# Softmax normaliser by a vector reciprocal, and the causal mask by a vector copy, in a recurrent attention and gMLP kernel

## The chip, the cores and the metric

The kernel runs on one core of a Trainium2 chip. The time is that of one execution on the device, in microseconds (us), as the median of several runs. Engine names in the profile: PE is TensorE (matmuls), PEld its weight loads, DVE is VectorE, ACT is ScalarE, POOL is GpSimd, SP is SyncE, which here only issues DMAs. PSUM is the memory that TensorE writes its products to; it has eight banks of 128 partitions by 512 float32.

## The reference

Two blocks run one after the other on x of shape (2048, 512). The first is attention over segments of 32 rows with a memory of 8 rows that is carried from segment to segment, so the 64 segments can only be computed in order:

```python
for s in range(64):
    h = concat([mem, xs])                      # 8 + 32 rows of 512
    q, k, v = h @ Wq, h @ Wk, h @ Wv           # 32 heads of 128
    scores = where(mask, q k^T * scale, -1e9)  # 40 x 40 per head
    o = (softmax(scores) @ v) @ Wo
    mem, out[s] = o[:8], o[8:]
```

The mask lets every key through for the 8 memory rows and is causal for the others. The second block is a gated MLP: a layer norm, a product with `w_in`, GELU, a layer norm of one half, a product with the 2048x2048 matrix `w_sp` over the rows, a gate, and a product with `w_out`. Both blocks add to their input.

## The kernel before

All instructions are recorded by an `Emitter` with one list for each engine. The order in which the Python code calls `pe`, `act`, `dve`, `pool` and `sp` is the order on that engine, and waits are derived from the tokens that an instruction reads and writes, among them one token for each PSUM bank (`PB(bank)`). So the order of work is written out by hand in the loop over `s`.

A step of that loop is one segment. The 32 heads are handled in two halves, `b` = 0 and 1. In one half, four groups of 32 partitions hold four heads each. A step goes like this:

- `QK` (L481) computes queries and keys of a half, `QK_evac` copies them from PSUM by ScalarE (L488) and transposes them by VectorE (L494 for queries, L497 for keys).
- `S_half` puts the scores of a half into bank 0 or 1 (`SBK`). It begins with four matmuls of an identity with the mask (L511), which start the accumulation. Sixteen matmuls for the segment's own keys (L520) and four for the memory's keys (L526) add to it.
- `sm_exp` (L534) computes E = exp(scale * score + 44) by ScalarE.
- `sm_sums` (L541, L546) multiplies E by a block of ones, so that every row of a head's block holds the sum over the keys, in the same bank (columns 224 to 383).
- `sm_ln` (L553) and `sm_rcp` (L557) form the reciprocal of these sums by ScalarE, as exp(-ln(sum)) with scale factors.
- `sm_norm` (L561, L566) multiplies E by it on VectorE, in two instructions.
- `V_half` (L575) computes the values of a half, in four quarters of four matmuls; `V_evac` copies them from PSUM, by VectorE for half 0 (L584), by ScalarE for half 1 (L582).
- Then a filler group follows, a piece of work for a later stage (L411, L430 or L735), which all steps have but one.
- `PV_half` (L592, L598) multiplies values and probabilities, half 0 then half 1, into banks 0, 1, 6 and 7; `cT_evac` (L611, L613) copies the result out. Below, PV(0) and PV(1) are the two halves.
- `Wo` (L625) applies the output matrix, and `mem_out` (L649, L654) turns the first 8 rows into the memory for the next step's `QK`. `WoX_mm` (L676) does the remaining rows of earlier segments.

`qx_copy` (L504) runs once in each step on GpSimd, behind the scores, and serves as a clock for the steps. In step 0 the values of the memory part are computed as well (`start_v`), between the scores and `V_half`.

Of the kernel before, what the change touches and what calls it, by code (L numbers as in the profile page):

```python
# [9 lines left out]
ACT = mybir.ActivationFunctionType  # L10
ALU = mybir.AluOpType
# [158 lines left out]
def fast_path(nc, st, keep, A_x, A_mem0, A_Wq, A_Wk, A_Wv, A_Wo, A_seg_len, B_w_in, B_w_sp, B_b_sp, B_w_out, out):  # L170
# [9 lines left out]
    DC = D // 128  # L180
# [7 lines left out]
    scale = float(DH) ** -0.5  # L188
    EPS = 1e-5
    SHIFT = 44.0  # L190
    NEG = -1.0e30
    RBIAS = 44.42
    LNS = 2.0 ** -64
    RK = math.exp(-RBIAS)

    em = Emitter(n_dma_sems=40)

# [27 lines left out]
    E_sb = sb("E_sb", [128, 2, 224], BF)  # L225
    R_sb = sb("R_sb", [128, 2, 160], F32)
# [7 lines left out]
    ident = sb("ident", [128, 128], BF)  # L234
    mask = sb("mask", [128, 224], BF)
# [30 lines left out]
    def PB(b):  # L266
        return ("ps", b)
# [4 lines left out]
    def pe(fn, **k):  # L272
        return em.add("pe", fn, **k)

    def act(fn, **k):
        return em.add("act", fn, **k)

    def dve(fn, **k):
        return em.add("dve", fn, **k)

    def pool(fn, **k):
        return em.add("pool", fn, **k)
# [40 lines left out]
    def late_consts():  # L323
        pool(lambda e: e.memset(ones[:], 0.0), writes=["ones"])
        pool(lambda e: e.memset(Sc[:], 0.0), writes=["Sc"])
        pool(lambda e: e.memset(mask[:], 0.0), writes=["mask"])
        for c in range(4):
            q = slice(32 * c, 32 * c + 32)
            pool(lambda e, q=q: e.memset(ones[q, q], 1.0), writes=["ones"])
            pool(lambda e, q=q: e.affine_select(out=G_sb[q, :], in_=onesrc[q, 0:M], pattern=[[-1, M]], compare_op=ALU.is_equal,  # L330
                                                fill=0.0, base=0, channel_multiplier=1), reads=["onesrc"], writes=["G"])
            pool(lambda e, q=q: e.affine_select(out=F_sb[q, :], in_=onesrc[q, 0:32], pattern=[[-1, 32]], compare_op=ALU.is_equal,
                                                fill=0.0, base=-M, channel_multiplier=1), reads=["onesrc"], writes=["F"])
            pool(lambda e, q=q: e.affine_select(
                out=Sc[q, :].rearrange("p (s r) -> p s r", r=32)[:, :, XM:32], in_=onesrc[q, 0:32].rearrange("p (s r) -> p s r", r=8),
                pattern=[[-8, 4], [-1, 8]], compare_op=ALU.is_equal, fill=0.0, base=0, channel_multiplier=1),
                reads=["onesrc"], writes=["Sc"])
            m1 = mask[q, 0:160].rearrange("p (g t) -> p g t", t=40)[:, :, 16:40]
            pool(lambda e, m1=m1: e.affine_select(out=m1, in_=m1, pattern=[[0, 4], [1, 24]], compare_op=ALU.is_ge,
                                                  fill=NEG, base=8, channel_multiplier=-1), reads=["mask"], writes=["mask"])  # L340
            m2 = mask[q, 160:224].rearrange("p (g t) -> p g t", t=16)
            pool(lambda e, m2=m2: e.affine_select(out=m2, in_=m2, pattern=[[-8, 4], [0, 16]], compare_op=ALU.is_ge,
                                                  fill=NEG, base=0, channel_multiplier=1), reads=["mask"], writes=["mask"])
            pool(lambda e, m2=m2: e.affine_select(out=m2, in_=m2, pattern=[[8, 4], [0, 16]], compare_op=ALU.is_ge,
                                                  fill=NEG, base=7, channel_multiplier=-1), reads=["mask"], writes=["mask"])
            m3 = m2[:, :, 0:8]
            pool(lambda e, m3=m3: e.affine_select(out=m3, in_=m3, pattern=[[8, 4], [1, 8]], compare_op=ALU.is_ge,
                                                  fill=NEG, base=0, channel_multiplier=-1), reads=["mask"], writes=["mask"])
# [136 lines left out]
    def QK_evac(s, b, mi):  # L485
        bank = QKB[(b, mi)]
        tb = mi
        act(lambda e: e.activation(out=Tst[:, tb, :].rearrange("p (hp i r) -> p hp i r", i=32, r=2),  # L488
                                   in_=ps[:, bank, :].rearrange("p (hp r i) -> p hp i r", r=2, i=32), func=ACT.Copy),
            reads=[PB(bank)], writes=[("T", tb)])  # L490
        src = Tst[:, tb, :].bitcast(U32)
        if mi == 0:
            dst = QT[:, b, :, :, :].rearrange("p hp q r -> p (hp q r)").bitcast(U32).rearrange("p (hp q) -> p hp q", hp=8)[:, :, 8:40]
            dve(lambda e: e.transpose(out=dst, in_=src), reads=[("T", tb)], writes=[("QT", b)])  # L494
        else:
            dst = KT[:, b, :, :, :].rearrange("p hp q r -> p (hp q r)").bitcast(U32)
            dve(lambda e: e.transpose(out=dst, in_=src), reads=[("T", tb)], writes=[("KT", b)])  # L497

    def qx_copy(s):
# [4 lines left out]
        pool(lambda e: e.tensor_copy(out=dst, in_=src), reads=[("QTx", buf, 0, i) for i in range(8)],  # L504
             writes=[("QTe", 0), ("QTe", 1)])

    def S_half(s, b):
        bank = SBK[b]
        for c in range(4):
            q = slice(32 * c, 32 * c + 32)  # L510
            pe(lambda e, q=q, c=c: e.matmul(ps[q, bank, 0:224], lhsT=ident[:, q], rhs=mask[:, :], start=True, stop=False,  # L511
                                            skip_group_check=True, tile_position=(0, 32 * c)),
               reads=["ident", "mask"], writes=[PB(bank)])
        j = s % CK
        buf = (s // CK) % 2
        rd = [("QT", b), ("KT", b), ("QTe", b)]
        for g in range(4):
            for c in range(4):
                hp, r = 2 * c + g // 2, g % 2
                pe(lambda e, hp=hp, r=r, c=c, g=g: e.matmul(  # L520
                    ps[32 * c:32 * c + 32, bank, g * 40:(g + 1) * 40], lhsT=KT[:, b, hp, :, r], rhs=QT[:, b, hp, :, r],
                    start=False, stop=(g == 3), skip_group_check=True, tile_position=(0, 32 * c)),
                    reads=rd, writes=[PB(bank)])
        for c in range(4):
            h0 = 16 * b + 4 * c
            pe(lambda e, c=c, h0=h0: e.matmul(  # L526
                ps[32 * c:32 * c + 32, bank, 160:224], lhsT=QTx[buf][:, 1, j, h0:h0 + 4, :].rearrange("p h k -> p (h k)"),
                rhs=QT[:, b, 2 * c:2 * c + 2, 0:16, :].rearrange("p hp q r -> p hp r q"),
                start=False, stop=True, skip_group_check=True, tile_position=(0, 32 * c)),
                reads=rd + [("QTx", buf, 1, i) for i in range(8)], writes=[PB(bank)])  # L530
# [17 lines left out]
                                            skip_group_check=True, tile_position=(0, 32 * c)),  # L548
               reads=[("Ex", b), "ones"], writes=[PB(bank)])

    def sm_ln(b):
        bank = SBK[b]
        act(lambda e: e.activation(out=R_sb[:, b, :], in_=ps[:, bank, 224:384], func=ACT.Ln, scale=LNS),  # L553
            reads=[PB(bank)], writes=[("R", b)])

    def sm_rcp(b):
        act(lambda e: e.activation(out=R_sb[:, b, :], in_=R_sb[:, b, :], func=ACT.Exp, scale=-1.0, bias=RBIAS),  # L557
            reads=[("R", b)], writes=[("R", b)])

    def sm_norm(b):  # L560
        dve(lambda e: e.scalar_tensor_tensor(out=E_sb[:, b, 0:160], in0=R_sb[:, b, :], scalar=RK, in1=E_sb[:, b, 0:160],  # L561
                                             op0=ALU.mult, op1=ALU.mult),
            reads=[("R", b), ("E", b)], writes=[("E", b)])
        ev = E_sb[:, b, 160:224].rearrange("p (g q) -> p g q", q=16)
        rv = R_sb[:, b, :].rearrange("p (g q) -> p g q", q=40)[:, :, 0:16]
        dve(lambda e: e.scalar_tensor_tensor(out=ev, in0=rv, scalar=RK, in1=ev, op0=ALU.mult, op1=ALU.mult),  # L566
            reads=[("R", b), ("Ex", b)], writes=[("Ex", b)])

    def V_half(s, b, dcs=range(DC)):
# [31 lines left out]
                start=False, stop=True, skip_group_check=True, tile_position=(32 * c, 0)),  # L601
                reads=[("Vx", xb), ("Ex", b)], writes=[PB(PVB[c])])

    UNSC = 2.0 ** -64


    def cT_evac(c, eng):
# [288 lines left out]
    for s in range(NSEG):  # L896
# [16 lines left out]
        QK(s, 0, 1, (0, 1))  # L913
        QK(s, 0, 0, (2, 3))
        QK_evac(s, 0, 0)
        QK(s, 0, 1, (2, 3))
        QK_evac(s, 0, 1)
        for mi in range(2):
            QK(s, 1, mi)
            lastop["qk"[mi]] = em.by_eng["pe"][-1]  # L920
            QK_evac(s, 1, mi)
        if s == 0:
            for n in range(2):
                start_v(n)
# [3 lines left out]
            for n in range(2, 4):  # L928
                start_v(n)
        V_half(s, 0)  # L930
        V_evac(0, "dve")
        sm_sums(0)
        sm_ln(0)
        S_half(s, 1)
        lastop["s"] = em.by_eng["pe"][-1]
        sm_exp(1)
        sm_rcp(0)
        if s == 0:
            for n in range(4, 8):
                start_v(n)  # L940
        V_half(s, 1, (0, 1, 2))
        sm_sums(1)
        sm_ln(1)
        sm_rcp(1)
        V_half(s, 1, (3,))
        lastop["v"] = em.by_eng["pe"][-1]
        if s == NSEG - 1:
            sp(lambda e: e.dma_start(w_in1, winr[:, :, 0:FH]), writes=["w_in1"], after=[lastop["s"], lastop["x"]])
            xn2T_dma(11, [lastop["s"], lastop["x"]])
            z2_back(0, 7, lastop["v"])  # L950
        V_evac(1, "act")
        sm_norm(0)
        sm_norm(1)
        if s + 1 < NSEG:
            qx_copy(s + 1)
            lastop["x"] = em.by_eng["pool"][-1]
# [1037 lines left out]
```

## Time and profile before

| what | value |
|---|---|
| median of 3 runs | 885.25 us |
| lowest and highest run | 884.95 and 886.3 us |
| the profiled execution, its own time | 887.59 us |
| the profiled execution, span of its instructions | 885.8 us |
| mean granted TensorE clock in it | 0.994 |

The profile is of one execution, and its span leaves out a little at both ends, so its own time is above its span and, here, the median of the unprofiled runs is slightly below the span. In the rows of a timeline the columns are: start in us, duration in us, engine, line, operation, output and inputs, and how many instructions were merged into the row; in brackets how long the engine was idle before it and what ended that. The duration of a merged row reaches from the first start to the last end. In a row of a group the numbers behind the bar are the total busy time in us and the mean duration in ns.

### The profile page before, as it was taken

What the parts mean: (1) busy time and instruction counts of PE and PEld (TensorE: products, weight loads), DVE (VectorE), ACT (ScalarE), POOL (GpSimd) and SP (SyncE); (2) the same over time, 40 slices, a digit from 0 to 9 for tenths busy, and PEclk for the clock granted to TensorE, in tenths of its full rate; (3) what the DMA queues carried; (4) which work ended last, traced back from release to release, by engine and by line L of the source; (5) the groups of instructions that cost most, each with busy time, mean ns of one, the idle gap of its engine ahead of it and who ended that gap; (6) DMA issues with size and microseconds to landing.
All of it is one profiled execution on the core that took longest, in us unless ns stands there. A gap on an engine that the chain in (4) does not pass through costs nothing.

```text
span 885.8 us, 46595 instructions
## 1 busy us (share of the span) xinstructions
PE 858.6 (97%) x21446; PEld 488.5 (55%) x21453; DVE 487.6 (55%) x1128; ACT 457.3 (52%) x1147; POOL 110.6 (12%) x280
## 2 busy tenths in 40 slices
PE   6889999999999999999999999999999998999997
PEld 6645555565566655656565555555555543444443
DVE  3445556565556556565655565556555557364343
ACT  2346565666665656666665666466665575400000
POOL 1420111111111111010101011111101013200000
PEclk9999999999999999999999999999999999999999
DMA  9962232123320311211312121523222299032101
GB/s 320 377 177 63 64 57 61 44 59 63 60 58 25 84 46 32 65 45 52 60 43 52 46 66 47 102 69 78 73 62 67 62 244 333 2 101 76 62 13 38
DMA packets 109210, 76.35 MB, mean 86 GB/s; under 512 B 64104, under 2 KB 94512, under 8 KB 109008
## 3 DMA queue, kind: packets, MB, share of 16 engines
q1 hardware_dynamic: 108496, 73.04, 30.1%
q8 instruction: 170, 2.79, 1.3%
q14 instruction: 32, 0.26, 0.1%
q0 software_dynamic: 192, 0.20, 0.1%
q10 hardware_dynamic: 320, 0.07, 0.0%
HBM read 41.75 MB, written 20.91 MB: 71 GB/s over the span
## 4 chain that ended last, share of the span: by engine, by line
PE 94%; DVE 2%; issue 1%; DMA 1%; POOL 1%; ACT 0%; DVEq 0%
PE f_ps L481 26%; PE f_ps L625 13%; PE f_ps L575 12%; PE f_ps L1099 11%; PE f_ps L411 7%; PE f_ps L676 4%; PE f_ps L592 3%; PE f_ps L430 3%; PE f_ps L1188 3%; PE f_ps L1092 2%; PE f_ps L735 2%; PE f_ps L520 2%; PE f_ps L541 1%; PE f_ps L511 1%; PE f_ps L649 1%
## 5 line engine op out<-in xcount | busy, mean ns | idle before, releaser
L481 PE MATMUL f_ps<-f_arena,f_hT 128*32 128x512 bf16 x4096 | 240.3, 380 | 0.5 <-issue 0.2
L488 ACT ACTIVATE f_Tst<-f_ps 128x512 bf16<-128x512 f32 x256 | 145.9, 596 | 78.1 <-PE f_ps L481 77.9
L481 PEld LDWEIGHTS f_ps<-f_arena,f_hT 128*32 128x32 bf16 x4096 | 92.9, 96 | 104.0 <-ACT f_hT L654 32.7
L575 PE MATMUL f_ps<-f_arena,f_hT 128*32 128x512 bf16 x2048 | 140.4, 378 | 0.0
L625 PE MATMUL f_ps<-f_arena,f_cT 128*32 128x256 bf16 x4096 | 129.2, 274 | 0.9 <-ACT f_cT L611 0.8
L625 PEld LDWEIGHTS f_ps<-f_arena,f_cT 128*32 128x32 bf16 x4096 | 101.2, 97 | 21.7 <-ACT f_cT L611 18.7
L494 DVE STREAM_TRANSPOSE f_QT<-f_Tst 128x256 uint32<-128x256 uint32 x128 | 57.0, 446 | 91.7 <-ACT f_Tst L488 91.7
L1099 PE MATMUL f_ps<-f_arena 128*128 128x512 bf16 x448 | 100.9, 382 | 0.0
L613 DVE TENSOR_SCALAR f_cT<-f_ps 128x320 bf16<-128x320 f32 x128 | 56.9, 487 | 41.2 <-PE f_ps L598 41.2
L1099 PEld LDWEIGHTS f_ps<-f_arena 128*128 128x128 bf16 x448 | 44.1, 99 | 53.9 <-issue 2.2
L497 DVE STREAM_TRANSPOSE f_KT<-f_Tst 128x256 uint32<-128x256 uint32 x128 | 57.0, 445 | 29.1 <-ACT f_Tst L488 26.4
L411 PE MATMUL f_ps<-f_hTe,f_arena 128*128 128x128 bf16 x1024 | 68.0, 225 | 4.0 <-DVE f_arena L422 2.9
L611 ACT ACTIVATE f_cT<-f_ps 128x320 bf16<-128x320 f32 x128 | 49.0, 435 | 38.4 <-PE f_ps L598 38.4
L411 PEld LDWEIGHTS f_ps<-f_hTe,f_arena 128*128 128x128 bf16 x1024 | 60.3, 101 | 14.1 <-issue 9.5
L504 POOL COPY f_QT<-f_arena 128x256 bf16<-128x256 bf16 x64 | 30.7, 479 | 298.2 <-PE f_ps L526 298.1
L561 DVE SCALAR_TENSOR_TENSOR f_E_sb<-f_R_sb,f_E_sb 128x160 bf16<-128x160 f32 x128 | 41.7, 325 | 46.2 <-ACT f_R_sb L557 46.2
L642 DVE CAST f_part<-f_ps 128x256 bf16<-128x256 f32 x64 | 27.2, 425 | 68.9 <-PE f_ps L625 68.9
L553 ACT ACTIVATE f_R_sb<-f_ps 128x160 f32<-128x160 f32 x128 | 39.0, 305 | 37.9 <-PE f_ps L546 37.9
L575 PEld LDWEIGHTS f_ps<-f_arena,f_hT 128*32 128x32 bf16 x2048 | 45.2, 95 | 21.1
L1105 DVE TENSOR_TENSOR f_arena<-f_ps,f_arena 128x512 f32<-128x512 f32 x28 | 19.3, 690 | 60.7 <-PE f_ps L1099 60.7
L654 ACT ACTIVATE f_hT<-f_ps 128x16 bf16<-128x16 f32 x126 | 23.2, 184 | 55.1 <-PE f_ps L649 54.7
L633 POOL COPY f_cTx<-f_cT 128x256 bf16<-128x256 bf16 x64 | 25.6, 400 | 197.1 <-DVE f_cT L613 197.1
(113 smaller groups left out, 1165.8 us busy)
## 6 DMA issues: line engine op xcount, KB each, us to landing
wT_d<-f_wst SPq DMA_DIRECT2D x32, 256.0 KB, 2.3
f_arena<-wT_d SPq DMA_DIRECT2D x32, 256.0 KB, 5.1
f_arena<-in_A_Wq_dram SPq DMA_DIRECT2D x4, 1024.0 KB, 8.8
f_arena<-in_A_Wk_dram SPq DMA_DIRECT2D x4, 1024.0 KB, 14.2
f_arena<-in_A_Wv_dram SPq DMA_DIRECT2D x4, 1024.0 KB, 14.8
f_arena<-in_A_Wo_dram SPq DMA_DIRECT2D x4, 1024.0 KB, 13.6
f_Vx<-vext_d SPq DMA_DIRECT2D x62, 64.0 KB, 2.8
vext_d<-f_Vs SPq DMA_DIRECT2D x24, 128.0 KB, 2.0
```

The costliest lines, as they stand in the source:

```text
L411: pe(lambda e, h=h, dc=dc, hh=hh: e.matmul(ps[:, bank, hh * 128:(hh + 1) * 128], lhsT=ws[:, dc, h * DH:(h + 1) * DH], rhs=hTe[:, ck % 3, d ...
L481: pe(lambda e, dc=dc, c=c, rhs=rhs: e.matmul(ps[32 * c:32 * c + 32, bank, :], lhsT=hT[:, sl, dc, :], rhs=rhs, start=(dc == 0), stop=(dc == ...
L488: act(lambda e: e.activation(out=Tst[:, tb, :].rearrange("p (hp i r) -> p hp i r", i=32, r=2), in_=ps[:, bank, :].rearrange("p (hp r i) -> ...
L494: dve(lambda e: e.transpose(out=dst, in_=src), reads=[("T", tb)], writes=[("QT", b)])
L497: dve(lambda e: e.transpose(out=dst, in_=src), reads=[("T", tb)], writes=[("KT", b)])
L553: act(lambda e: e.activation(out=R_sb[:, b, :], in_=ps[:, bank, 224:384], func=ACT.Ln, scale=LNS), reads=[PB(bank)], writes=[("R", b)])
L561: dve(lambda e: e.scalar_tensor_tensor(out=E_sb[:, b, 0:160], in0=R_sb[:, b, :], scalar=RK, in1=E_sb[:, b, 0:160], op0=ALU.mult, op1=ALU.m ...
L575: pe(lambda e, dc=dc, c=c, c0=c0: e.matmul(ps[32 * c:32 * c + 32, bank, :], lhsT=hT[:, sl, dc, :], rhs=w_v[:, dc, c0:c0 + 512], start=(dc ...
L611: act(lambda e: e.activation(out=dst, in_=src, func=ACT.Copy, scale=UNSC), reads=[PB(PVB[c])], writes=[("cT", c)])
L613: dve(lambda e: e.tensor_scalar(out=dst, in0=src, scalar1=UNSC, scalar2=None, op0=ALU.mult), reads=[PB(PVB[c])], writes=[("cT", c)])
L625: pe(lambda e, h=h, g=g, i=i, b=b, c=c: e.matmul(ps[32 * g:32 * g + 32, bank, 0:d1 - d0], lhsT=cTh[:, i, 8:40], rhs=w_o[:, h, d0:d1], star ...
L1099: pe(lambda e: e.matmul(ps[:, bank, 0:TB], lhsT=z2[:, sc, fb * 128:(fb + 1) * 128], rhs=wTb[tb % 2][:, :, sc, :], start=(n == 0), stop=(n ...
```

## The change

The reciprocal of the sums is taken by one VectorE instruction from PSUM in place of the two ScalarE functions. The scale factors go into the matrix of ones, and the normalisation becomes a plain product. Both halves' values are copied from PSUM by ScalarE. The mask is no longer brought in by matmuls: VectorE copies it into the score bank, half 0 behind that half's query transpose and half 1 behind the second half's query transpose, and all score matmuls add to it. The normalisation of a half stands directly behind its reciprocal. From step 1 on, the first quarter of `V_half` of half 1 runs ahead of the first sums, and the other three quarters ahead of the second sums; before, three quarters stood ahead of the second sums and one behind them.

```diff
-    RBIAS = 44.42
-    LNS = 2.0 ** -64
-    RK = math.exp(-RBIAS)
+    SUMS = 2.0 ** -40
+    UNSC = SUMS
...
-            pool(lambda e, q=q: e.memset(ones[q, q], 1.0), writes=["ones"])
+            pool(lambda e, q=q: e.memset(ones[q, q], SUMS), writes=["ones"])
...
+    def mask_put(b):
+        bank = SBK[b]
+        dve(lambda e: e.tensor_copy(out=ps[:, bank, 0:224], in_=mask[:, :]), reads=["mask"], writes=[PB(bank)])
+
     def S_half(s, b):
         bank = SBK[b]
-        for c in range(4):
-            q = slice(32 * c, 32 * c + 32)
-            pe(lambda e, q=q, c=c: e.matmul(ps[q, bank, 0:224], lhsT=ident[:, q], rhs=mask[:, :], start=True, stop=False,
-                                            skip_group_check=True, tile_position=(0, 32 * c)),
-               reads=["ident", "mask"], writes=[PB(bank)])
...
-    def sm_ln(b):
+    def sm_rcp(b):
         bank = SBK[b]
-        act(lambda e: e.activation(out=R_sb[:, b, :], in_=ps[:, bank, 224:384], func=ACT.Ln, scale=LNS),
-            reads=[PB(bank)], writes=[("R", b)])
-
-    def sm_rcp(b):
-        act(lambda e: e.activation(out=R_sb[:, b, :], in_=R_sb[:, b, :], func=ACT.Exp, scale=-1.0, bias=RBIAS),
-            reads=[("R", b)], writes=[("R", b)])
+        dve(lambda e: e.reciprocal(out=R_sb[:, b, :], in_=ps[:, bank, 224:384]), reads=[PB(bank)], writes=[("R", b)])
 
     def sm_norm(b):
-        dve(lambda e: e.scalar_tensor_tensor(out=E_sb[:, b, 0:160], in0=R_sb[:, b, :], scalar=RK, in1=E_sb[:, b, 0:160],
-                                             op0=ALU.mult, op1=ALU.mult),
+        dve(lambda e: e.tensor_tensor(out=E_sb[:, b, 0:160], in0=R_sb[:, b, :], in1=E_sb[:, b, 0:160], op=ALU.mult),
             reads=[("R", b), ("E", b)], writes=[("E", b)])
...
-        dve(lambda e: e.scalar_tensor_tensor(out=ev, in0=rv, scalar=RK, in1=ev, op0=ALU.mult, op1=ALU.mult),
+        dve(lambda e: e.tensor_tensor(out=ev, in0=rv, in1=ev, op=ALU.mult),
             reads=[("R", b), ("Ex", b)], writes=[("Ex", b)])
...
         QK_evac(s, 0, 0)
+        mask_put(0)
         QK(s, 0, 1, (2, 3))
         QK_evac(s, 0, 1)
         for mi in range(2):
             QK(s, 1, mi)
             lastop["qk"[mi]] = em.by_eng["pe"][-1]
             QK_evac(s, 1, mi)
+            if mi == 0:
+                mask_put(1)
...
         V_half(s, 0)
-        V_evac(0, "dve")
+        V_evac(0, "act")
+        if s > 0:
+            V_half(s, 1, (0,))
         sm_sums(0)
-        sm_ln(0)
+        sm_rcp(0)
         S_half(s, 1)
         lastop["s"] = em.by_eng["pe"][-1]
         sm_exp(1)
-        sm_rcp(0)
+        sm_norm(0)
...
-        V_half(s, 1, (0, 1, 2))
+        V_half(s, 1, (1, 2, 3) if s > 0 else range(DC))
         sm_sums(1)
-        sm_ln(1)
         sm_rcp(1)
-        V_half(s, 1, (3,))
+        sm_norm(1)
         lastop["v"] = em.by_eng["pe"][-1]
...
         V_evac(1, "act")
-        sm_norm(0)
-        sm_norm(1)
```

More of the change, by code (lines that the diff above doesn't have):

```diff
@@ L602, in PV_half @@
                 reads=[("Vx", xb), ("Ex", b)], writes=[PB(PVB[c])])
-    UNSC = 2.0 ** -64
     def cT_evac(c, eng):
```

## The prediction

> **What bounds the kernel now.** I read the page first, for which engine is full.
>
> ```profile
> span 885.8 us, 46595 instructions
> ## 1 busy us (share of the span) xinstructions
> PE 858.6 (97%) x21446; PEld 488.5 (55%) x21453; DVE 487.6 (55%) x1128; ACT 457.3 (52%) x1147; POOL 110.6 (12%) x280
> ```
>
> TensorE is busy for 97% of the span, and VectorE (DVE) and ScalarE (ACT) for about half. So work taken from TensorE is time, and work moved between the other two is free until TensorE has to wait for it. Which wait is near, an average can't say. For that I read one ordinary step in the timeline, one engine at a time: TensorE from the scores on, with most of the V and filler groups left out.
>
> ```profile
> 407.00 0.27 PE L511 MATMUL f_ps<-f_mask,f_ident 128*32 128x224 bf16 x4
> 407.10 0.27 PE L520 MATMUL f_ps<-f_QT,f_KT 128*32 128x40 bf16 x16
> 407.20 0.20 PE L526 MATMUL f_ps<-f_QT,f_arena 128*32 128x64 bf16 x4
> 407.23 1.03 PE L575 MATMUL f_ps<-f_arena,f_hT 128*32 128x512 bf16 x16
> 408.13 0.25 PE L541 MATMUL f_ps<-f_E_sb,f_ones 128*32 128x160 bf16 x4
> 408.21 0.20 PE L546 MATMUL f_ps<-f_E_sb,f_ones 128*32 128x64 bf16 x4
> 408.23 0.27 PE L511 MATMUL f_ps<-f_mask,f_ident 128*32 128x224 bf16 x4
> 408.36 0.28 PE L520 MATMUL f_ps<-f_QT,f_KT 128*32 128x40 bf16 x16
> ...
> 409.16 0.25 PE L541 MATMUL f_ps<-f_E_sb,f_ones 128*32 128x160 bf16 x4
> ...
> 410.84 0.28 PE L592 MATMUL f_ps<-f_E_sb,f_V_sb 32*128 32x40 bf16 x16
> ```
>
> A row's duration overlaps the next row, so a group costs the difference of two starts. No row here has an idle time in brackets: TensorE never waits in this stretch. The last row is the product of probabilities and V for the second half of the heads, PV(1). It needs the second half's normalised E. VectorE over the same time:
>
> ```profile
> 406.19 0.45 DVE L497 STREAM_TRANSPOSE f_KT<-f_Tst 128x256 uint32<-128x256 uint32 x1
> 407.00 0.45 DVE L494 STREAM_TRANSPOSE f_QT<-f_Tst 128x256 uint32<-128x256 uint32 x1 [0.36 <-ACT f_Tst L488]
> 407.86 0.45 DVE L497 STREAM_TRANSPOSE f_KT<-f_Tst 128x256 uint32<-128x256 uint32 x1 [0.42 <-ACT f_Tst L488]
> 408.32 0.69 DVE L584 CAST f_V_sb<-f_ps 128x512 bf16<-128x512 f32 x1
> 409.36 0.33 DVE L561 SCALAR_TENSOR_TENSOR f_E_sb<-f_R_sb,f_E_sb 128x160 bf16<-128x160 f32 x1 [0.35 <-ACT f_R_sb L557]
> 409.61 0.22 DVE L566 SCALAR_TENSOR_TENSOR f_E_sb<-f_R_sb,f_E_sb 128x64 bf16<-128x64 f32 x1
> 410.20 0.33 DVE L561 SCALAR_TENSOR_TENSOR f_E_sb<-f_R_sb,f_E_sb 128x160 bf16<-128x160 f32 x1 [0.37 <-ACT f_R_sb L557]
> 410.44 0.22 DVE L566 SCALAR_TENSOR_TENSOR f_E_sb<-f_R_sb,f_E_sb 128x64 bf16<-128x64 f32 x1
> ```
>
> The second normalisation's main part ends at 410.53 and PV(1) starts at 410.84: the softmax has some 0.3 us in hand in a step. That is all the room the change has on this chain. ScalarE's part of it:
>
> ```profile
> 408.46 0.30 ACT L553 ACTIVATE f_R_sb<-f_ps 128x160 f32<-128x160 f32 x1 [0.39 <-PE f_ps L546]
> 408.75 0.36 ACT L534 ACTIVATE f_E_sb<-f_ps 128x224 bf16<-128x224 f32 x1
> ...
> 410.07 0.58 ACT L582 ACTIVATE f_V_sb<-f_ps 128x512 bf16<-128x512 f32 x1
> ```
>
> **Mask.** Two L511 groups leave TensorE: 407.10 - 407.00 = 0.10 and 408.36 - 408.23 = 0.13, together 0.23 us a step, or 14.7 us over 64 steps. In their place VectorE makes two copies of 128x224. Their price comes from the groups of VectorE's instructions (mean ns behind the bar):
>
> ```profile
> L613 DVE TENSOR_SCALAR f_cT<-f_ps 128x320 bf16<-128x320 f32 x128 | 56.9, 487 | 41.2 <-PE f_ps L598 41.2
> L584 DVE CAST f_V_sb<-f_ps 128x512 bf16<-128x512 f32 x64 | 44.3, 692 | 1.2 <-PE f_ps L575 0.2
> L561 DVE SCALAR_TENSOR_TENSOR f_E_sb<-f_R_sb,f_E_sb 128x160 bf16<-128x160 f32 x128 | 41.7, 325 | 46.2 <-ACT f_R_sb L557 46.2
> ```
>
> From 160 to 512 elements the time grows by 367 ns, so one pass costs 1.043 ns an element and 158 ns besides; for 320 this gives 492, measured 487. A copy of 224 is then 0.39 us (0.27 if it took two elements at a time). The second one stands behind the query transpose that ends at 407.45 and ahead of the key transpose at 407.86, in idle time: free. The first pushes the first key transpose from 406.19 to about 406.55, so its end from 406.64 to 407.00, just where the scores would now start: 0 to 0.05 us, taken as 0. Both banks were read by ScalarE before the transposes in front of the copies, so the copies add no wait of their own.
>
> **V evacuation and V quarter.** VectorE loses the 0.69 of L584. ScalarE loses two L553 and two L557 a step and gains 0.58 (L582) between the two exps. The first V is ready 0.1 us earlier, so this copy runs from about 408.22 to 408.80 and the second exp starts at 408.80 in place of 408.75. The quarter of the V work pulled forward hides that: nothing. But it delays the first sums: sixteen L575 matmuls take 408.13 - 407.23 = 0.90, four take 0.22, so the first sums start at 408.13 - 0.10 + 0.22 = 408.25.
>
> **Reciprocal.** This term decides. L553 started 0.33 us after the first sums' matmul, so the reciprocal can start at 408.58. Call its time R. A handover between engines takes 0.05 (the exp ends at 409.11, the sums start at 409.16). The normalisation stays a product of the same shape, 0.33 and 0.22, with 0.47 from the first start to the second end. The second reciprocal is queued on VectorE behind the first normalisation, so both reciprocals lie on one chain: it starts at 408.58 + R + 0.05 + 0.47 = 409.10 + R. The second E is ready R + 0.05 + 0.33 later, and PV(1) can start at 409.10 + 2R + 0.38 + 0.05 = 409.53 + 2R. Today it starts at 410.84. So R below 0.65 us costs nothing, and each us above costs 2 us a step. Everything behind PV(1) on TensorE, which runs in order, waits with it: the evacuations of the context, Wo, and the next step's queries and keys.
>
> The trace has no reciprocal on VectorE. Bounds: the nearest row from below is one pass over 160 elements, L561, 0.325 us. From above there is no row, only the line: k passes cost 0.158 + 0.167k. In that line the break-even of 0.65 us is three passes. [...] I take eight passes, an estimate from that count and the line's slope: R = 0.158 + 1.333 = 1.49 us, and PV(1) starts at 412.51, 1.67 late in every step. This is 64 x 1.67 = 107 us.
>
> [...]
>
> **What the wait does to the clock.** TensorE's added idle time is 1.67 us and the 0.23 us of mask that is gone, 1.9 us a step around PV. One place shows what such idle time does. In the windows view (length, then PE busy; PEclk, DMA share and GB/s close the row):
>
> ```profile
> 49.30:52.70 3.40, 2.16 (x39) 0.96 (x32) 1.73 (x5) 1.55 (x4) 1.57 (x3) 1.00 1.07 295
> 52.70:56.10 3.40, 2.62 (x48) 1.94 (x45) 0.69 (x1) 0.60 (x1) 1.07 (x2) 1.00 0.67 152
> 554.50:557.90 3.40, 2.00 (x72) 0.98 (x63) 1.19 (x6) 1.78 (x6) 0.44 (x1) 1.00 1.28 215
> 557.90:561.30 3.40, 3.40 (x68) 2.44 (x64) 0.82 (x2) 1.01 (x3) 0.40 (x1) 0.50 1.36 175
> ```
>
> With 1.24 us idle in 3.4 the granted clock stayed at 1.00; after 1.40 us idle in 3.4 it was 0.50 for the next 3.4. This was the step without filler, and its length is seen between L504 copies:
>
> ```profile
> 544.13 0.47 POOL L504 COPY f_QT<-f_arena 128x256 bf16<-128x256 bf16 x1 [6.48 <-PE f_ps L526]
> ...
> 554.46 0.48 POOL L504 COPY f_QT<-f_arena 128x256 bf16<-128x256 bf16 x1 [2.44 <-PE f_ps L526]
> ...
> 567.77 0.47 POOL L504 COPY f_QT<-f_arena 128x256 bf16<-128x256 bf16 x1 [3.79 <-PE f_ps L526]
> ```
>
> 10.33 us before it, 13.31 with it: about 1.3 for the wait and 1.7 for half a clock over 3.4 us. With 1.9 us idle in each step I expect the same 1.7 us behind most waits, where TensorE is again the bound. A wait that straddles two stretches of 3.4 us is spared. But the step would be 10.33 + 1.67 + 1.70 = 13.70, four stretches of 3.4 within 0.1, so a wait that was caught finds the next one at the same place. I take 17 steps in 20: 64 x 0.85 x 1.70 = 92 us.
>
> [...]
>
> **Sum.** 885.8 + 107 + 92 = 1085 in span. The profiled run lies 1.8 us above its span, the median of the runs 0.5 below the span: 1084 us.
>
> **Rivals.** *A1, slow reciprocal, clock holds:* 885.8 + 107 - 0.5 = 992 us. For it: the wait is cut in two by PV(0), and windows at 49.30 and 52.70 stood 0.8 to 1.2 us idle. *B, faster:* the reciprocal is one pass or two, R up to 0.49. PV(1) could start at 410.51, TensorE comes there at 410.61, and the whole 0.23 us a step is kept: 885.2 - 14.7 = 870.5 us. It decides at R = 0.65; for it speaks that every VectorE row here lies on the one-pass line. [...] *C, three to six passes:* each pass above three costs 2 x 0.167 x 64 = 21 us, so 885 at three and about 950 at six, the clock holding. *D, the first key transpose* is late by the whole 0.39 us copy: 64 x 0.35 = 22 us, but under a slow reciprocal it only adds.
>
> **How the numbers follow.** The forecast (slow reciprocal, clock falls) has 0.58, A1 0.20, B 0.12, C 0.08 with 0.02 of it at no change, and 0.02 lies above all. Range: A1 with seven passes is 992 - 21 = 971; the forecast with the clock falling in every step is 885.3 + 64 x 3.37 = 1101. With a little at both ends, 965 to 1105 holds the forecast and A1 with the upper part of C, 8 in 10. Faster: 0.12 (B). Same, within the 0.2% that a measurement can tell: 0.02. Slower: 0.86.
>
> **What would show it.** A reciprocal row with mean near 1490 ns x128; a wait of PE L592 for the normalisation in about every step, 1.6 us or more; rows of 0.50 in the clock, and L504 copies 13.6 to 13.7 us apart. Copies 12.0 apart with a clock of 1.00 mean A1. If the reciprocal's mean is below 650 ns, the forecast is wrong at its root and TensorE should be as full as before. Right in any case: no L511 mask groups, 128 copies of the mask near 390 ns, and PE L520 with no wait for a transpose longer than 0.1 us.

## The result, and the profile after

The changed kernel takes 943.45 us (median of six runs, 942.82 to 946.61) against 884.92 us (six runs, 882.82 to 886.3) for the kernel before on the same chip: a ratio of 1.067, 95% interval 1.065 to 1.0689. The forecast was 1084 us, 965 to 1105. The direction was right; the time lies 22 us below the lower end.

The page of the changed kernel: span, busy time of the engines, and the chain that ended last, by engine.

```profile
span 944.8 us, 45514 instructions
PE 857.5 (91%) x20941; PEld 487.5 (52%) x20941; DVE 615.3 (65%) x1320; ACT 424.3 (45%) x955; POOL 110.2 (12%) x280
PE 73%; DVE 22%; issue 2%; DMA 1%; POOL 1%; ACT 0%; DVEq 0%
```

TensorE was 97% busy and is 91% busy: it waits now, though it has 512 mask matmuls less to do. VectorE holds 22% of the chain that ended last. The groups of VectorE's instructions and the waits (total us, times, longest us) give the price and the place:

```profile
L551 DVE RECIPROCAL f_R_sb<-f_ps 128x160 f32<-128x160 f32 x128 | 147.8, 1154 | 15.9 <-PE f_ps L544 15.9
L508 DVE CAST f_ps<-f_mask 128x224 f32<-128x224 bf16 x128 | 47.0, 367 | 0.0
PE f_ps L584 <- DVE f_R_sb L551: 52.8, 63, 1.0
```

The reciprocal takes 1154 ns where 1490 was forecast, the mask copy 367 where 390 was. PV waits for the reciprocal in 63 of 64 steps, 52.8 us in all. One ordinary step, TensorE in the timeline:

```profile
427.92 0.27 PE L518 MATMUL f_ps<-f_QT,f_KT 128*32 128x40 bf16 x16
428.06 1.25 PE L567 MATMUL f_ps<-f_arena,f_hT 128*32 128x512 bf16 x20
429.13 0.24 PE L539 MATMUL f_ps<-f_E_sb,f_ones 128*32 128x160 bf16 x4
...
431.29 0.19 PE L584 MATMUL f_ps<-f_E_sb,f_V_sb 32*128 32x40 bf16 x1
432.24 0.27 PE L584 MATMUL f_ps<-f_E_sb,f_V_sb 32*128 32x40 bf16 x15 [0.76 <-DVE f_R_sb L551]
...
432.69 0.28 PE L584 MATMUL f_ps<-f_E_sb,f_V_sb 32*128 32x40 bf16 x16
```

and VectorE over the same time:

```profile
...
429.46 1.16 DVE L551 RECIPROCAL f_R_sb<-f_ps 128x160 f32<-128x160 f32 x1 [0.24 <-PE f_ps L544]
430.65 0.33 DVE L554 TENSOR_TENSOR f_E_sb<-f_R_sb,f_E_sb 128x160 bf16<-128x160 f32 x1
430.90 0.22 DVE L558 TENSOR_TENSOR f_E_sb<-f_R_sb,f_E_sb 128x64 bf16<-128x64 f32 x1
431.03 1.15 DVE L551 RECIPROCAL f_R_sb<-f_ps 128x160 f32<-128x160 f32 x1
432.22 0.32 DVE L554 TENSOR_TENSOR f_E_sb<-f_R_sb,f_E_sb 128x160 bf16<-128x160 f32 x1
```

VectorE is in one piece of work from 429.46 on: reciprocal, normalisation, reciprocal, normalisation. On TensorE, from the first row of the scores (the mask group in the kernel before) to PV(1) it was 410.84 - 407.00 = 3.84 us before, and is 432.69 - 427.92 = 4.77 us now: 0.93 a step. Times 64 this is 59.5 us; the spans differ by 944.8 - 885.8 = 59.0. Added up over all 64 steps of both traces, the stretch from the first scores to PV(1) grows by 58.9 us. The whole loss lies on this one stretch.

PV(0) is cut in two. Its first matmul goes at 431.29; its second writes bank 1, which holds the second half's sums, and waits until the second reciprocal has read them (431.03 + 1.15 = 432.18). So TensorE stands idle 0.76 us there, with the idle time named in brackets.

### The profile page after: what moved, and what is told of

The parts are those of the page before. It is cut to its first block, busy times and chain, and to the rows that moved or that the text cites. A ratio compares the mean times of both kernels' runs of the same rounds, so it can differ in the third digit from the quotient of the medians.

```text
span 944.8 us, 45514 instructions
## 1 busy us (share of the span) xinstructions
PE 857.5 (91%) x20941; PEld 487.5 (52%) x20941; DVE 615.3 (65%) x1320; ACT 424.3 (45%) x955; POOL 110.2 (12%) x280
## 4 chain that ended last, share of the span: by engine, by line
PE 73%; DVE 22%; issue 2%; DMA 1%; POOL 1%; ACT 0%; DVEq 0%
PE f_ps L480 24%; DVE f_R_sb L551 15%; PE f_ps L616 12%; PE f_ps L1092 10%; PE f_ps L567 7%; PE f_ps L667 4%; PE f_ps L1181 3%; DVE f_E_sb L558 2%; DVE f_E_sb L554 2%; PE f_ps L410 2%; PE f_ps L1085 2%; PE f_ps L429 2%; PE f_ps L584 2%; PE f_ps L640 1%; DVE f_st L1067 1%
## 5 line engine op out<-in xcount | busy, mean ns | idle before, releaser
L480 PE MATMUL f_ps<-f_arena,f_hT 128*32 128x512 bf16 x4096 | 240.6, 380 | 0.1
L551 DVE RECIPROCAL f_R_sb<-f_ps 128x160 f32<-128x160 f32 x128 | 147.8, 1154 | 15.9 <-PE f_ps L544 15.9
L567 PE MATMUL f_ps<-f_arena,f_hT 128*32 128x512 bf16 x2048 | 133.0, 378 | 0.0
L584 PE MATMUL f_ps<-f_E_sb,f_V_sb 32*128 32x40 bf16 x2048 | 46.8, 178 | 62.5 <-DVE f_R_sb L551 52.8
L574 ACT ACTIVATE f_V_sb<-f_ps 128x512 bf16<-128x512 f32 x128 | 76.4, 597 | 29.1 <-PE f_ps L567 20.7
L584 PEld LDWEIGHTS f_ps<-f_E_sb,f_V_sb 32*128 32x128 bf16 x2048 | 29.2, 91 | 87.9 <-DVE f_R_sb L551 58.9
## 6 DMA issues: line engine op xcount, KB each, us to landing
f_arena<-in_A_Wv_dram SPq DMA_DIRECT2D x4, 1024.0 KB, 14.7
```

The source lines that it names most:

```text
L480: pe(lambda e, dc=dc, c=c, rhs=rhs: e.matmul(ps[32 * c:32 * c + 32, bank, :], lhsT=hT[:, sl, dc, :], rhs=rhs, start=(dc == 0), stop=(dc == ...
L551: dve(lambda e: e.reciprocal(out=R_sb[:, b, :], in_=ps[:, bank, 224:384]), reads=[PB(bank)], writes=[("R", b)])
L567: pe(lambda e, dc=dc, c=c, c0=c0: e.matmul(ps[32 * c:32 * c + 32, bank, :], lhsT=hT[:, sl, dc, :], rhs=w_v[:, dc, c0:c0 + 512], start=(dc ...
L574: act(lambda e: e.activation(out=V_sb[:, b, :], in_=ps[:, bank, :], func=ACT.Copy), reads=[PB(bank)], writes=[("V", b)])
L584: pe(lambda e, q=q, c=c, g=g, c0=c0: e.matmul(ps[:, PVB[c], c0:c0 + 40], lhsT=V_sb[q, b, g * 128:(g + 1) * 128], rhs=E_sb[q, b, g * 40:(g ...
```

## The experiments

The theory: the two reciprocals lie in series behind the first sums, so that every microsecond of R (the time of one reciprocal) above about 0.65 costs 2 us a step, and nothing else of the change costs time. Against it stand: another part of the change (the mask copies, the order of V, the wait on bank 1) carries some of the loss; or TensorE's clock does. Ratios are to the kernel before on the same chip, whose median was 882.5 to 883.3 us there.

**The reciprocal replaced by one pass.** The division is left out; the instruction reads and writes the same elements.

```diff
-e.reciprocal(out=R_sb[:, b, :], in_=ps[:, bank, 224:384])
+e.tensor_scalar(out=R_sb[:, b, :], in0=ps[:, bank, 224:384], scalar1=0.0, scalar2=2.14e-9, op0=ALU.mult, op1=ALU.add)
```

> The changed kernel with the reciprocal replaced by one pass of VectorE over the same 160 columns (a constant in place of the division, so the division is left out; everything else stays, the read of the same score bank included). Theory 1, the whole loss is the length of the two reciprocals (1.154 us each, on one chain): at 0.33 us each the chain ends before TensorE gets there, the mask's 0.23 us a step is kept, and the time is 885 - 14.7, about 870 us, with no wait of L584 on VectorE. Theory 2, the loss comes from the order on VectorE and from the banks (mask copies, V copies on ScalarE, PV(0) waiting for the read of bank 1): these are all still there, so the time stays clearly above 885, some 900 to 935 us.

Measured 863.95 us, ratio 0.9797 (0.9769 to 0.9825). The group of that line and PV in the timeline:

```profile
L551 DVE TENSOR_SCALAR f_R_sb<-f_ps 128x160 f32<-128x160 f32 x128 | 41.6, 325 | 15.9 <-PE f_ps L544 15.8
411.36 0.27 PE L585 MATMUL f_ps<-f_E_sb,f_V_sb 32*128 32x40 bf16 x16
...
411.50 0.28 PE L585 MATMUL f_ps<-f_E_sb,f_V_sb 32*128 32x40 bf16 x16
```

With everything else of the change in place, the loss becomes a gain: no other part of it costs 59 us. PV(0) runs in one piece again. The gain on the kernel before is 18.7 us where 14.7 was expected, and the time 6 us below the 870. Part of it is in the distance of PV(0) and PV(1). Here it is 0.14 us; in the same place of the kernel before it was 0.25:

```profile
410.59 0.27 PE L592 MATMUL f_ps<-f_E_sb,f_V_sb 32*128 32x40 bf16 x16
410.71 0.21 PE L598 MATMUL f_ps<-f_E_sb,f_Vx 32*128 32x64 bf16 x4
410.84 0.28 PE L592 MATMUL f_ps<-f_E_sb,f_V_sb 32*128 32x40 bf16 x16
```

So before, PV(1) came 0.11 us later behind PV(0) than the work between them takes, without an idle time in brackets, as the row of L598 overlaps the gap. Added up over the 64 steps, the distance is 22.0 us before and 11.4 here. What took the 0.11 us is not shown: in the rows of before, the main part of the normalised E (410.53) and the copied V (410.07 + 0.58 = 410.65) were both ready well ahead of 410.84.

**Half the columns.** The division is done for 80 of the 160 sums of each partition; a constant written once stands for the others.

```diff
-e.reciprocal(out=R_sb[:, b, :], in_=ps[:, bank, 224:384])
+e.reciprocal(out=R_sb[:, b, 0:80], in_=ps[:, bank, 224:304])
```

> The changed kernel with the reciprocal over 80 of the 160 columns (the other 80 columns are multiplied by a constant, so half of the division is left out). Theory 1 with six passes: 1154 ns for 160 is 154 + 160 x 6.25, so 80 columns should take 654 ns; PV(1) then moves 1.0 us forward against the changed kernel, that is 0.07 ahead of the kernel before: 943.5 - 64 x 1.0 = 879 us, near the break-even that was predicted at 0.65 us. If the reciprocal's price is mostly fixed and not by element, its row stays near 1.1 us and the time near 940 us.

Measured 881.1 us, ratio 0.9986 (0.997 to 1.0002), with this row:

```profile
L552 DVE RECIPROCAL f_R_sb<-f_ps 128x80 f32<-128x80 f32 x128 | 83.7, 654 | 16.0 <-PE f_ps L545 16.0
```

At R = 0.654 the kernel ties with the one before: the break-even of 0.65 us holds.

**More columns: R near the forecast's 1.49.** The reciprocal reads 213 columns of the bank; the 53 more are not used.

```diff
-e.reciprocal(out=R_sb[:, b, :], in_=ps[:, bank, 224:384])
+e.reciprocal(out=R_sb[:, b, :], in_=ps[:, bank, 224:437])
```

> The changed kernel with the reciprocal over 213 columns (53 of no use), so that it lasts 154 + 213 x 6.25 = 1485 ns, the length that the prediction took. The chain grows by 2 x 0.33 us a step. Theory 'the clock holds' (the waits are cut in two by PV(0) and no 3.4 us stretch stands idle for 1.4): 943.5 + 64 x 0.66 = 986 us, granted clock near 0.99. Theory 'the clock falls' of the prediction: idle time near 1.6 us a step, the clock at 0.50 behind most waits, 1.7 us more in most steps: about 1080 us, mean granted clock near 0.9.

Measured 1039.88 us (median of five executions, 1021.83 to 1044.27), a ratio of 1.158 to 1.183 from one execution to the other: between the two. In the profiled execution, the one of 1021.83 us, its reciprocals, the wait of PV for them (total us, times, longest us), and stretches of 3.41 us in the windows view (length, busy time of PE, PEld, DVE, ACT and POOL, granted clock, DMA share, GB/s):

```profile
L551 DVE RECIPROCAL f_R_sb<-f_ps 128x213 f32<-128x213 f32 x128 | 190.8, 1490 | 15.9 <-PE f_ps L544 15.9
PE f_ps L584 <- DVE f_R_sb L551: 85.1, 63, 1.4
104.56:107.97 3.41, 1.76 (x60) 0.74 (x52) 2.90 (x8) 0.58 (x3) 0.00 (x0) 1.00 0.00 0
107.97:111.38 3.41, 3.41 (x80) 2.79 (x76) 1.07 (x3) 0.66 (x2) 0.40 (x1) 0.50 0.28 59
...
118.21:121.62 3.41, 1.76 (x60) 0.78 (x56) 2.90 (x8) 0.58 (x3) 0.00 (x0) 1.00 0.00 0
121.62:125.03 3.41, 3.41 (x76) 2.70 (x76) 1.02 (x3) 0.70 (x4) 0.40 (x1) 0.50 0.19 41
...
261.57:264.98 3.41, 1.90 (x73) 1.27 (x76) 2.94 (x7) 1.03 (x3) 0.01 (x1) 1.00 0.02 5
264.98:268.39 3.41, 3.41 (x76) 2.33 (x68) 1.16 (x3) 0.90 (x3) 0.39 (x1) 0.50 0.40 93
...
739.44:742.85 3.41, 1.80 (x56) 0.72 (x44) 3.34 (x6) 0.85 (x2) 0.40 (x1) 1.00 0.01 2
742.85:746.26 3.41, 3.27 (x134) 2.50 (x128) 1.91 (x6) 1.43 (x5) 0.40 (x1) 1.00 0.12 41
```

A stretch with 3.41 - 1.76 = 1.65 us idle was followed by one at clock 0.50, and so was one with 1.51; one with 1.61 was not. The clock's record has 25 such stretches at 0.50 in the loop. The first ten, from 80.66 on, come 118.21 - 104.56 = 13.65 us apart, which is the locking that the forecast foresaw, but it does not last. With the forecast's R the clock fell in 25 of 64 steps of that execution, not in 17 of 20.

The other executions were longer as their mean granted clock was lower: 0.956 in the profiled one of 1021.83 us, 0.943 in that of 1035.11 and 0.936 in that of 1044.27. A mean of 0.936 over a span of 1042.5 us makes (1 - 0.936) x 1042.5 / (0.5 x 3.41) = 39 stretches at half clock, where 0.956 over 1020.0 makes 26. Each costs up to half of 3.41, 1.7 us, so the 13 more are an estimate of 22 us, the distance between the two times.

**Between them: 186 columns.** The same edit with `224:410`.

> The changed kernel with the reciprocal over 186 columns (26 of no use): 154 + 186 x 6.25 = 1317 ns. The chain grows by 2 x 0.16 us a step, the idle time of a step from about 1.0 to 1.3 us, below the 1.4 to 1.5 us at which the clock was seen to fall. So the clock should hold near 0.99 and the time be 943.5 + 64 x 0.33 = 964 us. If the clock falls here too: 1000 us or more, mean clock below 0.97.

```profile
L551 DVE RECIPROCAL f_R_sb<-f_ps 128x186 f32<-128x186 f32 x128 | 168.6, 1317 | 15.9 <-PE f_ps L544 15.9
```

Measured 967.66 us, ratio 1.0937 (1.09 to 1.0973). Two us a step for each us of R would be 64 x 2 x 0.163 = 21 us above the changed kernel; the execution with the highest clock (0.996, 963.13 us) lies 20 above it. The profiled one (0.988, 971.31 us) has six stretches at 0.50 in its loop, so the clock begins to cost something here.

**The mask by matmuls again, the rest of the change kept.** The four matmuls of `S_half` are put back, both calls of `mask_put` taken out.

```diff
     def S_half(s, b):
         bank = SBK[b]
+        for c in range(4):
+            pe(... e.matmul(ps[q, bank, 0:224], lhsT=ident[:, q], rhs=mask[:, :], ...))
...
-        mask_put(0)
...
-                mask_put(1)
```

> The changed kernel with one part undone: the mask comes in by TensorE matmuls again and not by the VectorE copy. Theory 'the chain through the reciprocals is the bound': the first half's group of 0.10 us delays the first sums and so the chain, the second half's 0.13 us lies behind the first sums in TensorE's idle time: 943.5 + 64 x 0.10 = 950 us. Rival, TensorE's total is still what counts: 943.5 + 14.7 = 958 us. Rival, the copies cost more on VectorE than they save: below 943 us.

Measured 949.28 us, ratio 1.0753 (1.0722 to 1.0784). Taking the mask from TensorE is worth 949.28 - 943.45 = 6 us here (8 when the kernel before of the same chip is taken off each). That fits the first L511 group alone (0.10 us x 64 = 6.4): the second one, behind the first sums, stands beside the reciprocals, and by the chain it costs nothing.

**The mask by VectorE alone, all else as before.** The opposite edit, on the kernel before.

> The kernel before with one part alone: the mask copied by VectorE, nothing else changed (reciprocal by ScalarE, V order as before). Theory 1: the copy itself is free, but the second half's scores cannot start before that half's key transpose ends (408.31 in the step that was read) and TensorE would now come there 0.2 us too early, so the gain turns into a wait of L518's like in front of the second half: 885 us or at most 6 us less. Theory 2, TensorE's work alone counts: 885 - 14.7 = 870 us.

Measured 883.09 us, ratio 1.0003 (0.9986 to 1.0021). The mask groups have gone, and nothing is gained. Rows of one step, of TensorE, VectorE and ScalarE:

```profile
408.62 0.25 PE L540 MATMUL f_ps<-f_E_sb,f_ones 128*32 128x160 bf16 x4
...
408.86 0.28 PE L519 MATMUL f_ps<-f_QT,f_KT 128*32 128x40 bf16 x16
...
407.86 0.36 DVE L509 CAST f_ps<-f_mask 128x224 f32<-128x224 bf16 x1
408.36 0.45 DVE L497 STREAM_TRANSPOSE f_KT<-f_Tst 128x256 uint32<-128x256 uint32 x1
...
407.73 0.60 ACT L488 ACTIVATE f_Tst<-f_ps 128x512 bf16<-128x512 f32 x1 [0.27 <-PE f_ps L481]
```

The second scores used to follow the first sums by way of the mask group. Now they start at 408.86, behind the second key transpose (408.36 + 0.45 = 408.81). That transpose waits for ScalarE's copy of the keys (407.73 + 0.60 = 408.33), as it did before; the mask copy ahead of it was over at 408.22. So the second scores stand as far behind the first (407.50) as before: 1.36 us.

**Mask by VectorE and the V quarter ahead of the first sums, reciprocal by ScalarE.** The edit of the last experiment, and `V_half` of half 1 ordered as in the change.

```diff
+        if s > 0:
+            V_half(s, 1, (0,))
         sm_sums(0)
...
-        V_half(s, 1, (0, 1, 2))
+        V_half(s, 1, (1, 2, 3) if s > 0 else range(DC))
```

> The kernel before with the mask copied by VectorE and the first quarter of the second half's V ahead of the first sums; the reciprocal stays on ScalarE. Theory 1: the quarter fills the wait for the key transpose, so most of the mask's 0.23 us a step becomes time, limited by ScalarE's chain behind the second sums (ln, exp, V copy end at about the same time as before): 870 to 876 us, faster than both kernels. Theory 2, no gain without the lighter ScalarE queue: 882 to 886 us.

Measured 882.39 us, ratio 0.9993 (0.9978 to 1.0008): a miss. TensorE's second scores and PV(1), and ScalarE between them:

```profile
406.85 0.28 PE L519 MATMUL f_ps<-f_QT,f_KT 128*32 128x40 bf16 x16
408.87 0.27 PE L591 MATMUL f_ps<-f_E_sb,f_V_sb 32*128 32x40 bf16 x16
409.29 0.28 PE L591 MATMUL f_ps<-f_E_sb,f_V_sb 32*128 32x40 bf16 x16
...
407.24 0.36 ACT L533 ACTIVATE f_E_sb<-f_ps 128x224 bf16<-128x224 f32 x1
407.49 0.33 ACT L556 ACTIVATE f_R_sb<-f_R_sb 128x160 f32<-128x160 f32 x1
407.99 0.30 ACT L552 ACTIVATE f_R_sb<-f_ps 128x160 f32<-128x160 f32 x1 [0.17 <-PE f_ps L545]
408.32 0.34 ACT L556 ACTIVATE f_R_sb<-f_R_sb 128x160 f32<-128x160 f32 x1
408.56 0.58 ACT L581 ACTIVATE f_V_sb<-f_ps 128x512 bf16<-128x512 f32 x1
```

From the second scores to the end of the V copy it takes 409.14 - 406.85 = 2.29 us, as it did before (408.36 to 410.07 + 0.58 = 410.65). PV(1) waits for that copy and stands 0.42 us behind PV(0). (The waits view names L565, the second part of VectorE's normalisation, which ends 0.01 us behind the copy. By the code the first matmul of PV(1) needs only the first part, which was over at 409.01.) So the kernel before had two limits close together: TensorE, and ScalarE's exp, exp of -ln, ln, exp of -ln and V copy behind the second scores.

**The V products into bank 1 last.** Of `PV_half`, the 12 matmuls for the other banks go first, which takes the wait on bank 1 behind them.

```diff
-        for g in range(4):
-            for c in range(4):
+        for g, c in [(g, c) for g in range(4) for c in (0, 2, 3)] + [(g, 1) for g in range(4)]:
```

> The changed kernel with another order inside PV_half: the twelve products into banks 0, 6 and 7 first, the four into bank 1 last. In the changed kernel PV(0)'s second product waits for the second reciprocal, which reads bank 1. Theory 'that wait only takes the place of PV(1)'s wait for the second E': PV(0) is over earlier, PV(1) starts up to 0.09 us earlier: 0 to 6 us less than the changed kernel, 937 to 943 us. Theory 'the bank is the bound': the 0.76 us wait of a step goes, 900 to 915 us.

```profile
421.64 0.27 PE L583 MATMUL f_ps<-f_E_sb,f_V_sb 32*128 32x40 bf16 x12
422.61 0.19 PE L583 MATMUL f_ps<-f_E_sb,f_V_sb 32*128 32x40 bf16 x1 [0.69 <-DVE f_R_sb L551]
...
423.06 0.27 PE L583 MATMUL f_ps<-f_E_sb,f_V_sb 32*128 32x40 bf16 x14
```

Measured 946.86 us, ratio 1.071 (1.0682 to 1.0738): neither of the two. Twelve matmuls go ahead of the wait instead of one, and it is no faster. The wait on bank 1 only stands where the wait of PV(1) for the second E would stand, which comes out of the same chain of VectorE.

**The reciprocal alone, all else as before.** Mask by matmuls, V copy of half 0 on VectorE, V in the old order. The normalisation of a half stands directly behind its reciprocal, as in the change.

```diff
-activation(out=R_sb[:, b, :], in_=ps[:, bank, 224:384], func=ACT.Ln, scale=LNS)
-activation(out=R_sb[:, b, :], in_=R_sb[:, b, :], func=ACT.Exp, scale=-1.0, bias=RBIAS)
+e.reciprocal(out=R_sb[:, b, :], in_=ps[:, bank, 224:384])
```

> The kernel before with one part alone: the reciprocal on VectorE, the first V still copied by VectorE ahead of it, mask by TensorE, V order as before. Theory 1, one chain of VectorE instructions: the V copy (0.69) keeps the first reciprocal until about 409.0, two reciprocals and two normalisations follow, PV(1) starts near 412.1 in place of 410.84: 885 + 64 x 1.28 = 967 us, and more (up to 1000) if the clock falls behind some of the waits of 1.3 us. If the V copy is hidden: 885 + 64 x 0.75 = 933 us.

Measured 969.11 us, ratio 1.0963 (1.093 to 1.0997). The reciprocal alone loses 86 us; the other parts of the change win 26 of them back. If the parts add up, 6 to 8 are the mask's, by the experiment above. The rest comes with the V copy, which stood on VectorE directly ahead of the first reciprocal in this kernel's trace, and with the order of V; these two were not run apart. The clock fell twice in this loop, behind no more idle time than this:

```profile
92.01:95.42 3.41, 2.05 (x76) 1.17 (x72) 2.94 (x8) 0.92 (x3) 0.04 (x1) 1.00 0.02 5
95.42:98.83 3.41, 3.41 (x80) 2.10 (x72) 0.92 (x2) 0.57 (x2) 0.36 (x1) 0.50 0.37 100
```

That is 3.41 - 2.05 = 1.36 us.

**The changed kernel again**, beside the others.

> The changed kernel itself, beside the others of this set: about 943 us where the kernel before takes 885, a ratio of 1.067.

Measured 942.93 us, ratio 1.0676 (1.0649 to 1.0702).

**One pass, and the mask by matmuls.** The division is left out as in the first experiment, and the mask comes back to TensorE: what is the lighter softmax chain worth without the mask?

> The kernel one_pass (a one-pass constant in place of the reciprocal, the division left out) with the mask brought in by TensorE again. It has the lighter ScalarE queue and no saved TensorE work. Theory 'both are needed' (TensorE and the chain through ScalarE were each near the step's length before): 885 less 0 to 0.11 us a step for the closer PV(0) and PV(1), 876 to 885 us. Theory 'the shorter softmax carries the gain': 864 to 870 us.

Measured 873.95 us, ratio 0.9889 (0.9864 to 0.9913), 2 us below the first band. The shorter chain alone is worth 9 us, the mask on top of it 873.95 - 863.95 = 10 us (9 against the kernel before of the same chip), and the mask without it, as shown above, nothing.

**One half on each engine.** The reciprocal of half 0 stays on VectorE; that of half 1 goes back to ScalarE as exp(-ln(sum)).

```diff
+    def sm_rcp_act(b):
+        act(... activation(out=R_sb[:, b, :], in_=ps[:, bank, 224:384], func=ACT.Ln) ...)
+        act(... activation(out=R_sb[:, b, :], in_=R_sb[:, b, :], func=ACT.Exp, scale=-1.0) ...)
...
-        sm_rcp(1)
+        sm_rcp_act(1)
```

> The changed kernel with the first half's reciprocal on VectorE and the second half's on ScalarE (ln, then exp of the negative). The first half's 1.15 us then lies beside the second half's scores, exp and V, the second half's takes 0.65 us as before, and the two no longer follow one another. Theory 1: the second E is ready about 1.0 us earlier than in the changed kernel, within 0.1 to 0.2 us of TensorE: 870 to 878 us. If VectorE's queue is too full (the first half's reciprocal late for PV(0)): 885 to 900 us.

Measured 874.61 us, ratio 0.9904 (0.9876 to 0.9931): faster than both kernels. Its PV and the V copy ahead of PV(1):

```profile
415.07 0.27 PE L589 MATMUL f_ps<-f_E_sb,f_V_sb 32*128 32x40 bf16 x16
...
415.41 0.27 PE L589 MATMUL f_ps<-f_E_sb,f_V_sb 32*128 32x40 bf16 x16
...
414.77 0.58 ACT L579 ACTIVATE f_V_sb<-f_ps 128x512 bf16<-128x512 f32 x1
```

Only one reciprocal lies on VectorE's chain, and two functions are gone from ScalarE's. PV(0) runs whole, PV(1) stands 0.34 us behind it, right behind the V copy (415.35). That copy is what is late next.

## Why the prediction was wrong, and where it was right

**The chain was right.** Put at the place of the forecast's step (scores at 427.92 against 407.00, so 20.92 less), the first sums start at 408.21 (forecast 408.25), the first reciprocal at 408.54 (408.58), and PV(1) at 411.77. The forecast's 409.53 + 2R with the measured R is 411.84. Two small errors in it nearly cancel: the second reciprocal starts 0.14 us earlier than written, and PV(1) starts 0.15 us behind the second normalisation's main part, not 0.05. Laid out by R, with 64 x 2 x (R - 0.65) on 885.3 us:

| R, us | forecast's formula, clock at full speed | measured, us |
|---|---|---|
| 0.654 | 886 | 881.1 |
| 1.154 (the change) | 950 | 943.45 |
| 1.317 | 971 | 967.66 |
| 1.490 (the forecast's R) | 993 | 1039.88 (1021.83 to 1044.27) |

**The step that failed is the size of R.** The line of 0.158 + 0.167k was right, k was 6 and not 8. No run shows the eight passes: they were the author's estimate. The four measured sizes give (1154 - 654) / 80 = 6.25 ns an element and 154 ns besides, six times the 1.043 ns of one pass. An error of 0.34 us in R is 43 us in the sum. By which steps the division is worked out, no run here shows; they show its time, that of six passes.

**The clock step fell with it, and was too high in itself.** It is the larger part of the miss: of the 141 us between 1084 and 943, 92 are the clock's, 43 are R's, and 6 lie between the formula and the measured time. The 92 us rested on 1.9 us of idle time a step. With R at 1.154 the same count is 2 x (1.154 - 0.65) + 0.23 = 1.2 us, and the forecast's own row of 1.24 us had the clock hold. In the changed kernel an ordinary step's stretch and the one behind it, and one of the two in the loop that lowered the clock (the other lies in the first steps, 55.11 to 58.52), read:

```profile
430.58:433.99 3.41, 2.50 (x82) 1.79 (x83) 2.91 (x9) 1.07 (x3) 0.00 (x0) 1.00 0.07 20
433.99:437.40 3.41, 3.41 (x108) 1.99 (x104) 2.27 (x6) 0.87 (x4) 0.40 (x1) 1.00 0.02 5
...
601.24:604.65 3.41, 1.68 (x61) 0.96 (x65) 2.90 (x8) 1.19 (x3) 0.00 (x0) 1.00 1.11 209
604.65:608.06 3.41, 3.41 (x76) 2.23 (x64) 0.46 (x2) 0.57 (x2) 0.40 (x1) 0.50 0.58 159
```

0.91 us idle left the clock at 1.00, 1.73 idle halved it. That a wait across two stretches is spared, as the forecast has it, shows once, behind the changed kernel's loop: of the 2.15 us that TensorE waited for VectorE's L1048 (up to 797.60), 0.34 lay in the stretch up to 795.79 and 1.81 in the next, and the clock stayed at 1.00. In the kernel before, the same wait of 2.15 us lay in one stretch (735.37 to 738.78, 2.11 us idle), and the stretch behind it was at 0.50. At R = 1.49 the clock does fall, but the median was 1040 us: 47 above the formula with the clock holding, half of the 92.

**The cases.** What happened is rival C at six passes, "about 950", to which the forecast gave 0.08 in all. The range was meant to take in the upper part of C, but C at six passes lies below its lower end of 965: that was an error of the range, apart from R. Case A1's mechanism (the clock holds) came out, at another R. Rival B was right about its point of decision, 0.65 us, and its time of 870.5 us was 6 too high, as one pass gave 863.95: "TensorE never waits" overlooked the 0.11 us ahead of PV(1). Rival D did not come: the first scores start at 427.92 with no idle time ahead of them.

**The covers.** The mask copies and the V copy on ScalarE cost nothing that shows, as forecast: with one pass in place of the division all of them are there, and the kernel gains. That PV(0) goes ahead and cuts the wait in two did not come: one matmul of it goes, not all, with no effect on the time. "Work taken from TensorE is time" was only half right: the mask's 14.7 us came as 0, 6 or 10 us, according to what else limited the step. What stays open is why the clock held behind the 1.61 us of 739.44 and fell behind the 1.51 of 261.57 and the 1.36 of the run with the reciprocal alone.

## What to carry to other kernels

An instruction whose cost no row shows should first be placed: how often it lies on one chain, and at what duration the chain becomes the limit. Here that point (0.65 us) held and the duration did not, so the range should have followed the duration through every value that was thought possible, each with its own clock. And where an engine is full but another chain ends only just behind it, work taken off the one gives little until the other is shortened as well; a split of the reciprocals between two engines gained here what neither engine gave alone.

## What the runs showed of the hardware

VectorE's reciprocal of float32 from PSUM took 654, 1154, 1317 and 1490 ns for 80, 160, 186 and 213 columns: about 6.3 ns a column and some 154 ns besides, where one pass over 160 took 325 ns in all. TensorE's granted clock went to 0.50 for 3.41 us behind stretches of 3.41 us in which idle times of 1.36 us or more added up (1.36 with the reciprocal alone, 1.51 and 1.65 with 213 columns, 1.73 in the changed kernel), while the longest single wait for the reciprocal was 1.4 us, with 213 columns. The amount does not decide alone: behind 1.61 us in the loop with 213 columns, and behind 1.81 us at 795.79 in the changed kernel, the clock held. The least idle time read ahead of a fall is the 1.36 us.
